# Softmax sums in two parts and subtractions in three, set between dependent additions; logarithms two tiles later

## Chip, cores, metric

One NeuronCore of a Trainium2 chip. The time is device microseconds (us) of one execution; lower is better. A program on one core has no second die to compare with, so a run counts as slow when it lies over 1.5% above the fastest of the same kernel.

## The reference

```python
# dynamic convolution: x (8, 4160, 192), weight_gen (8, 4160, 8 heads, 7 taps)
w = softmax(weight_gen, axis=-1)                    # over the 7 taps
out[b, s, h, :] = sum over k of w[b, s, h, k] * x_pad[b, s + k, h, :]
# then, on the 33280 rows x of 192:
h1, h2 = x @ w1, x @ w2                             # 192 -> 1024
return np.maximum(h1, h2) @ w_out                   # 1024 -> 192
```

## The kernel before

The 260 rows of each partition are 17 batches (the last has 4 rows). A batch is worked off in units of 8 rows (the first two and the last batch in units of 4). TensorE (PE) takes a unit of 8 rows in 8 tiles, each with an eighth of the hidden layer. Per unit, VectorE (DVE) multiplies the 7 shifted copies of x by the weights and adds the 7 products in three steps; a transposing DMA turns the result y_t into yt; PE makes the hidden layer and the output from it; ScalarE (ACT) does the Relu, evacuates, and makes the weights as exp(w - ln(sum of exp w)). So each batch also needs one sum over the taps (`red`) and one subtraction of its logarithm (`shift`) on DVE, and one `ln` and three exponentials on ACT.

```python
    def red(b):                                   # L132: 896 fp32 elements to 128
        ...
        nc.vector.reduce_sum(out=s_ts[b], in_=_sub(e_ts.pop(b), 0, [[K, TH], [1, K]]), axis=AX.X)
    def ln(b):                                    # L135, ScalarE
        nc.scalar.activation(out=s_ts[b], in_=s_ts[b], func=AF.Ln)
    def shift(b):                                 # L140: 896 fp32 elements
        ...
        nc.vector.tensor_tensor(out=w_t, in0=w_t, in1=..., op=ALU.subtract)
    def adds(b, o, first=False):                  # L172, L177, L179: each reads what the one before wrote
        ...
        nc.vector.tensor_tensor(out=taps(0, 1, 3), in0=taps(0, 1, 3), in1=taps(3, 1, 3), op=ALU.add)
        ...
        nc.vector.tensor_tensor(out=taps(0, 2, 2), in0=taps(0, 2, 2), in1=taps(1, 5, 2), op=ALU.add)
        nc.vector.tensor_tensor(out=_sub(y_ts[b], ...), in0=taps(0, 1, 1), in1=taps(2, 1, 1), op=ALU.add)
    ...
    def extra(t):                                 # what goes with tile t of PE; s = its place in the batch
        if s == 0 and b + 1 < NB:
            mul(c, 0); shift(c + 1); adds(c, 0)   # c = b + 1
        if s == 8 and b + 2 < NB:
            mul(b + 1, 8); red(b + 3); adds(b + 1, 8)
        ...
        for o, at in ((0, 8), (8, 12)):           # the two exponentials that make the weights
            c = (t - at) // 16 + 2
            if (t - at) % 16 == 0 and ...: weights(c, o)
        if s == 14 and 3 < b + 3 < NB:
            ln(b + 3)
        c = (t - 4) // 16 + 3                     # the exponential ahead of the sums
        if (t - 4) % 16 == 0 and 3 < c < NB:
            exp_sum(c)
```

PE takes its tiles in groups of three. An even group evacuates four results and calls `extra` between its Relus ("large" below); an odd one evacuates two and calls it at its end ("small").

The softmax here doesn't subtract the row's maximum and nothing guards it: scores larger than these inputs give would overflow.

Of the kernel before, what the change touches and what calls it, by code (L numbers as in the profile page):

```python
# [9 lines left out]
FP32 = mybir.dt.float32  # L10
# [4 lines left out]
AX = mybir.AxisListType  # L15


def _sub(base: bass.AP, off: int, dims):
    ap = [list(base.ap[0])] + [[int(s), int(c)] for s, c in dims]
    return dataclasses.replace(base, offset=base.offset + off, ap=ap)  # L20
# [3 lines left out]
def kernel(  # L24
# [9 lines left out]
    nc = tc.nc  # L34

    B, S, D = x.shape
    H, K = weight_gen.shape[2], weight_gen.shape[3]
    F = moe_w1.shape[1]
    P = 128
# [9 lines left out]
    BATCHES = [(c, min(16, CPP - c)) for c in range(0, CPP, 16)]  # L49
    NB = len(BATCHES)  # L50


    def pieces(b):
        n = BATCHES[b][1]
        at, done = [], 0
        for w in (4, 4, 4, 4) if b < 2 else (8, 8) if n == 16 else (n,):
            at.append((done, w))
            done += w
        return at
# [18 lines left out]
    psm = ctx.enter_context(tc.tile_pool(name="psm", bufs=3))  # L78
# [19 lines left out]
    wg_ts, xb_ts, e_ts, s_ts, en_ts, y_ts, yt_ts = {}, {}, {}, {}, {}, {}, {}  # L98
# [26 lines left out]
    def exp_sum(b):  # L125
        e_ts[b] = pe_.tile([P, BATCHES[b][1] * WGC], FP32, name="e_t", tag="e")
        nc.scalar.activation(out=e_ts[b], in_=wg_ts[b], func=AF.Exp)  # L127

    def red(b):
        TH = BATCHES[b][1] * H  # L130
        s_ts[b] = psm.tile([P, TH], FP32, name="sum_t", tag="sum")
        nc.vector.reduce_sum(out=s_ts[b], in_=_sub(e_ts.pop(b), 0, [[K, TH], [1, K]]), axis=AX.X)  # L132

    def ln(b):
        nc.scalar.activation(out=s_ts[b], in_=s_ts[b], func=AF.Ln)  # L135

    def shift(b):
        TH = BATCHES[b][1] * H
        w_t = _sub(wg_ts[b], 0, [[K, TH], [1, K]])
        nc.vector.tensor_tensor(out=w_t, in0=w_t, in1=_sub(s_ts.pop(b), 0, [[1, TH], [0, K]]),  # L140
                                op=ALU.subtract)

    def weights(b, o):

        N = dict(pieces(b))[o] * H
        if b not in en_ts:
            en_ts[b] = pen.tile([P, 16 * WGC * 2], BF16, name="en_t", tag="en")
        nc.scalar.activation(  # L148
            out=_sub(en_ts[b], o * WGC * 2, [[2 * N, K], [2, N], [1, 2]]),
            in_=_sub(wg_ts[b], o * WGC, [[1, K], [K, N], [0, 2]]), func=AF.Exp,  # L150
        )


    def mul(b, o):

        n = dict(pieces(b))[o]
        nc.vector.tensor_tensor(  # L157
            out=m_t[:, K * o * D:K * (o + n) * D],
            in0=_sub(xb_ts[b], o * D, [[D, K], [1, n * D]]),
            in1=_sub(en_ts[b], o * WGC * 2, [[2, K * n * H], [0, G // 2], [1, 2]]),  # L160
            op=ALU.mult,
        )

    def adds(b, o, first=False):

        w = dict(pieces(b))[o]
        n = w * D

        def taps(at, step, cnt):
            return _sub(m_t, K * o * D + at * n, [[step * n, cnt], [1, w * D]])  # L170

        nc.vector.tensor_tensor(out=taps(0, 1, 3), in0=taps(0, 1, 3), in1=taps(3, 1, 3), op=ALU.add)  # L172
        if first:
            return
        if b not in y_ts:
            y_ts[b] = py.tile([P, 16 * D], BF16, name="y_t", tag="y")
        nc.vector.tensor_tensor(out=taps(0, 2, 2), in0=taps(0, 2, 2), in1=taps(1, 5, 2), op=ALU.add)  # L177

        nc.vector.tensor_tensor(  # L179
            out=_sub(y_ts[b], o * D, [[64, 2], [P, 3 * w // 2], [1, 64]]),  # L180
            in0=taps(0, 1, 1), in1=taps(2, 1, 1), op=ALU.add,
        )

    def transpose(u):

        b, o, n = UNITS[u]
        yt = pyt.tile([P, 8 // 2 * 3 * P], BF16, name="yt", tag="yt")
        nc.sync.dma_start_transpose(
            out=yt[:, 0:n // 2 * 3 * P].rearrange("p (b t) -> p b t", t=P),
            in_=y_ts[b][:, o * D:(o + n) * D],  # L190
        )
        yt_ts[u] = yt

        nc.gpsimd.tensor_copy(out=gate, in_=yt[:, 0:1])  # L194
        c = b + 1 if o == 0 else b + 2
        if o == 8 and c < NB:
            load_x(c, 0, min(8, BATCHES[c][1]))
        if o == 0 and c < NB and BATCHES[c][1] > 8:
            load_x(c, 8, BATCHES[c][1] - 8)
        if o == 0 and b + 3 < NB:  # L200
            load_wg(b + 3, nc.gpsimd)
# [167 lines left out]
    OUTS, c = [[], [], []], 0  # L369
    for g in range(3, len(GROUPS)):  # L370
        most = 4 if g == 3 else 2 if GROUPS[g][1] == 2 or len(OUTS[-1]) == 4 else 4
        n = min(most, ready[g] - c)
# [80 lines left out]
    with tc.tile_pool(name="pstage", bufs=1) as pstage:  # L453
# [7 lines left out]
        for p0, p1, eng in ((16, P, nc.sync), (1, 16, nc.gpsimd)):  # L461
            eng.dma_start(
                out=xs[p0:p1, 0:PAD * D],
                in_=bass.AP(tensor=x.tensor, offset=(p0 * CPP - PAD) * D,
                            ap=[[CPP * D, p1 - p0], [1, PAD * D]]),
# [30 lines left out]
        nc.vector.tensor_copy(out=ident, in_=ident_f)  # L496
        exp_sum(0)
        red(0)
        ln(0)
        shift(0)  # L500
        xb_ts[0] = pxb.tile([P, (16 + PAD) * D], BF16, name="xb_t", tag="xb")
        nc.scalar.activation(out=xb_ts[0][:, 0:PAD * D], in_=xs[:, 0:PAD * D], func=AF.Copy,
                             scale=msk[:, 0:1])
        for o in (0, 4, 8, 12):
            weights(0, o)
        nc.vector.tensor_copy(out=xb_ts[0][:, PAD * D:(PAD + 4) * D],
                              in_=xs[:, PAD * D:(PAD + 4) * D])
# [5 lines left out]
        def w_diff(h, copy):  # L513
# [15 lines left out]
            out=wo[:, :].rearrange("p (f d) -> p f d", d=D),  # L529
            in_=bass.AP(tensor=moe_w_out.tensor, offset=0, ap=[[D, P], [P * D, FCH], [1, D]]),  # L530
# [39 lines left out]
        w_diff(1, nc.vector.tensor_copy)  # L570
        mul(0, 8)
        adds(0, 8, True)
        sum_transpose(1)
        exp_sum(1)
        red(1)
        hidden(1)
        ln(1)
        shift(1)
        mul(0, 12)
        tp = w1_transposed()  # L580
# [22 lines left out]
        weights(1, 4)  # L603
        mul(1, 0)
        adds(1, 0, True)
        sum_transpose(2, LEFT)
        load_x(2, 0, 16)
# [3 lines left out]
        w10_product()  # L611
        exp_sum(2)
        red(2)
        adds(1, 4, True)
        sum_transpose(3)
        weights(1, 8)
# [6 lines left out]
    def rest_of_1():  # L623
        mul(1, 8)
        shift(2)
        adds(1, 8, True)
        mul(1, 12)
# [16 lines left out]
    def extra(t):  # L644

        u, k = TILES[t]
        b, o, n = UNITS[u]
        s = o + k
        if s == 0 and b + 1 < NB:

            c = b + 1
            mul(c, 0)
            if c + 1 < NB:
                shift(c + 1)
            adds(c, 0)
        if s == 8 and b + 2 < NB:
            mul(b + 1, 8)
            if b + 3 < NB:
                red(b + 3)
            adds(b + 1, 8)  # L660
        if k == n // 4 - 1 and 7 < u + 1 < NU:
            transpose(u + 1)

        for o, at in ((0, 8), (8, 12)):
            c = (t - at) // 16 + 2
            if (t - at) % 16 == 0 and 2 < c < NB and o in dict(pieces(c)):
                weights(c, o)
        if s == 14 and 3 < b + 3 < NB:
            ln(b + 3)
        c = (t - 4) // 16 + 3  # L670
        if (t - 4) % 16 == 0 and 3 < c < NB:
            exp_sum(c)
# [7 lines left out]
    for g in range(4, len(GROUPS)):  # L680
        if GROUPS[g][1] == 3 and "c" not in ps:
            later_ps()
        tiles = [t for t in range(GROUPS[g][0], sum(GROUPS[g])) if t >= 16]
        if g in early:
            hidden(g, OUTS[g], early[g][0])
            early[g][1]()
            for t in tiles:
                extra(t)
        else:
            hidden(g, OUTS[g], beside=lambda: [extra(t) for t in tiles])  # L690
# [30 lines left out]
```

## Time and profile before

418.81 us median of 4 runs (418.5 to 419.28); profiled span 417.0 us.

| | busy us | ends |
|---|---|---|
| TensorE (PE) | 403.7 | with the kernel |
| VectorE (DVE), last y_t | 378.0 | 385.07 us |
| ScalarE (ACT) | 359.8 | with the kernel |

A high busy share on three engines does not tell which sets the time. The chain of work that ended last is followed back from the end; at each step it goes to what released an instruction, or to the one before it on its engine. On the kernel before it stayed on DVE:

```profile
DVE 73%; PE 17%; issue 4%; ACT 3%; DMA 2%; SPq 1%; DVEq 0%
```

### The profile page before, as it was taken

To read this page: it belongs to the slowest core of one execution; us is meant where nothing else is said; L and a number is where in the kernel's file an instruction comes from. 1 tells how busy PE (TensorE), PEld (TensorE's weight loads), DVE (VectorE), ACT (ScalarE), POOL (GpSimd) and SP (SyncE) were. 2 spreads that over 40 slices of the span, in tenths; PEclk is the share of its full clock that TensorE was granted. 3 is DMA by queue.
4 is the path that set the end of the run, shared out by engine and by line. 5 is a ranking of instruction groups with operands and counts; after the bars stand their busy time and mean duration, and the time that the engine had idled before them with its cause. 6 is when DMAs were issued, how large, how long until landed. Compare 5 with 4: busy or idle time off the path is not lost.

```text
span 417.0 us, 15881 instructions
## 1 busy us (share of the span) xinstructions
PE 403.7 (97%) x7369; PEld 326.8 (78%) x7369; DVE 378.0 (91%) x177; ACT 359.8 (86%) x416; POOL 69.0 (17%) x102
## 2 busy tenths in 40 slices
PE   7989999999999999999999999999999999999995
PEld 7878899777777778777787777877778677777795
DVE  5999999999999999999999999999999999999000
ACT  5898989999999899898989899899998898887871
POOL 1510101221201122212112232200113221120000
PEclk9999999999999999999999999999999999999999
DMA  8965427867569756875866669557674787685213
GB/s 235 260 168 169 108 68 169 183 153 129 144 151 181 192 151 163 207 147 153 201 149 147 168 127 242 142 163 198 142 209 64 165 202 151 128 163 115 97 49 144
DMA packets 60242, 65.68 MB, mean 157 GB/s; under 512 B 47601, under 2 KB 48497, under 8 KB 60176
## 3 DMA queue, kind: packets, MB, share of 16 engines
q0 software_dynamic: 8128, 24.11, 28.3%
q1 hardware_dynamic: 46720, 15.30, 21.5%
q10 hardware_dynamic: 5328, 25.27, 15.8%
q8 instruction: 57, 0.93, 0.9%
q14 instruction: 9, 0.07, 0.1%
HBM read 35.96 MB, written 25.56 MB: 148 GB/s over the span
## 4 chain that ended last, share of the span: by engine, by line
DVE 73%; PE 17%; issue 4%; ACT 3%; DMA 2%; SPq 1%; DVEq 0%
DVE m_t L157 36%; DVE m_t L172 15%; DVE m_t L177 11%; PE op_ps L290 8%; PE hd L250 5%; DVE sum_t L132 3%; DVE y_t L179 3%; DVE wg_t L140 3%; DMA ws1T<-in_moe_w_dram 2%; PE op_ps L302 2%; ACT rd_t L260 1%; PE hdp L250 1%; PE yps L218 1%; ACT en_t L148 0%; SPq L480 0%
## 5 line engine op out<-in xcount | busy, mean ns | idle before, releaser
L260 ACT ACTIVATE rd_t<-hd 128x1024 bf16<-128x1024 f32 (+1 forms) x206 | 234.6, 1183 | 30.8 <-PE hd L250 30.3
L290 PE MATMUL op_ps<-wo,rd_t 64*128 64x192 bf16 x4160 | 210.3, 243 | 0.1
L290 PEld LDWEIGHTS <-rd_t 64*128 64x128 bf16 x4160 | 180.1, 94 | 16.2 <-ACTq L323 0.3
L250 PE MATMUL hd<-yt,wd 64*128 64x512 bf16 (+1 forms) x1584 | 187.2, 360 | 1.1 <-ACT rd_t L260 0.9
L157 DVE TENSOR_TENSOR m_t<-xb_t,en_t 128x10752 bf16<-128x10752 bf16 (+1 forms) x37 | 187.5, 5070 | 0.2 <-ACT en_t L148 0.2
L250 PEld LDWEIGHTS <-wd 64*128 64x128 bf16 x1776 | 92.8, 94 | 42.3 <-issue 1.4
L194 POOL CAST gate<-yt 128x1 f32<-128x1 bf16 x29 | 33.2, 1146 | 280.8 <-DMA yt<-y_t 280.8
L172 DVE TENSOR_TENSOR m_t<-m_t 128x4608 bf16<-128x4608 bf16 (+1 forms) x34 | 79.5, 2339 | 0.1
L346 ACT COPY o_t<-op_ps 128x384 f32<-128x384 f32 (+1 forms) x99 | 56.9, 585 | 8.2 <-PE op_ps L290 8.1
L302 PE MATMUL op_ps<-w,yt 64*128 64x192 bf16 x780 | 55.3, 243 | 3.2 <-ACT o_t L346 2.5
L302 PEld LDWEIGHTS <-yt 64*128 64x128 bf16 x780 | 38.6, 94 | 20.1 <-issue 5.6
L177 DVE TENSOR_TENSOR m_t<-m_t 128x3072 bf16<-128x3072 bf16 (+1 forms) x29 | 50.2, 1730 | 1.0
L148 ACT ACTIVATE en_t<-wg_t 128x896 bf16<-128x896 f32 (+1 forms) x37 | 34.1, 935 | 1.9 <-ACT o_t L346 1.2
L179 DVE TENSOR_TENSOR y_t<-m_t 128x1536 bf16<-128x1536 bf16 (+1 forms) x29 | 27.4, 944 | 1.0
L336 DVE COPY o_t<-op_ps 128x192 f32<-128x192 f32 x1 | 0.4, 358 | 27.9 <-ACT o_t L336 27.9
L115 POOL DMA_DIRECT2D xb_t<-in_x_dram x32 | 17.2, 539 | 24.8 <-DVE m_t L157 16.1
L132 DVE TENSOR_REDUCE sum_t<-e_t 128x128 f32<-128x896 f32 (+1 forms) x17 | 17.6, 1037 | 2.9 <-ACT e_t L127 2.9
L127 ACT ACTIVATE e_t<-wg_t 128x896 f32<-128x896 f32 (+1 forms) x17 | 15.8, 928 | 3.3 <-DMA wg_t<-in_weight_gen_dram 2.8
L140 DVE TENSOR_TENSOR wg_t<-wg_t,sum_t 128x896 f32<-128x896 f32 (+1 forms) x17 | 17.7, 1043 | 0.8 <-ACT sum_t L135 0.8
L260 ACT ACTIVATE rd_t<-hdp 128x1024 bf16<-128x1024 f32 x16 | 15.7, 1027 | 1.5 <-PE hdp L250 0.5
L218 PE MATMUL yps<-ident,m_t 128*64 128x128 bf16 x492 | 15.3, 220 | 0.3 <-DVE m_t L157 0.2
L218 PEld LDWEIGHTS <-m_t 128*64 128x64 bf16 x492 | 14.1, 110 | 1.9 <-issue 1.1
(45 smaller groups left out, 85.6 us busy)
## 6 DMA issues: line engine op xcount, KB each, us to landing
out_dram<-o_t ACTq DMA_DIRECT2D x28, 768.0 KB, 4.3
xb_t<-in_x_dram POOLq DMA_DIRECT2D x28, 384.0 KB, 4.9
wg_t<-in_weight_gen_dram POOLq DMA_DIRECT2D x14, 448.0 KB, 6.3
xb_t<-xb_t POOLq DMA_DIRECT2D x16, 288.0 KB, 5.4
out_dram<-o_t ACTq DMA_DIRECT2D x8, 384.0 KB, 3.2
wg_t<-in_weight_gen_dram SPq DMA_DIRECT2D x2, 448.0 KB, 5.3
xs<-in_x_dram SPq DMA_DIRECT2D x2, 384.0 KB, 6.8
xb_t<-in_x_dram POOLq DMA_DIRECT2D x1, 768.0 KB, 6.8
```

The costliest lines, as they stand in the source:

```text
L148: nc.scalar.activation(out=_sub(en_ts[b], o * WGC * 2, [[2 * N, K], [2, N], [1, 2]]), in_=_sub(wg_ts[b], o * WGC, [[1, K], [K, N], [0, 2]] ...
L157: nc.vector.tensor_tensor(out=m_t[:, K * o * D:K * (o + n) * D], in0=_sub(xb_ts[b], o * D, [[D, K], [1, n * D]]), in1=_sub(en_ts[b], o * W ...
L172: nc.vector.tensor_tensor(out=taps(0, 1, 3), in0=taps(0, 1, 3), in1=taps(3, 1, 3), op=ALU.add)
L177: nc.vector.tensor_tensor(out=taps(0, 2, 2), in0=taps(0, 2, 2), in1=taps(1, 5, 2), op=ALU.add)
L179: nc.vector.tensor_tensor(out=_sub(y_ts[b], o * D, [[64, 2], [P, 3 * w // 2], [1, 64]]), in0=taps(0, 1, 1), in1=taps(2, 1, 1), op=ALU.add,)
L194: nc.gpsimd.tensor_copy(out=gate, in_=yt[:, 0:1])
L218: nc.tensor.matmul(yps[half(j), k * P:(k + 1) * P], lhsT=m_t[:, at:at + 64], rhs=ident, start=(t == taps[0]), stop=(t == taps[-1]), skip_g ...
L250: nc.tensor.matmul(hid_out(t, f, j), lhsT=wd[half(j), s * F + f * P:s * F + (f + 1) * P], rhs=_sub(yt_ts[u][half(j), :], (s + j) % 3 * P, ...
L260: nc.scalar.activation(out=rd[:, k * 1024:(k + n) * 1024], in_=hd[:, at:at + n * 1024], func=AF.Relu)
L290: return nc.tensor.matmul(op_out(c), lhsT=rd[half(r), k * 1024 + at:k * 1024 + at + P], rhs=wo[half(r), f * D:(f + 1) * D], start=False, s ...
L302: nc.tensor.matmul(op_out(c + j), lhsT=yt_ts[u][half(j), (3 * i + (s + j) % 3) * P:(3 * i + (s + j) % 3 + 1) * P], rhs=w10[half(j), s * D: ...
L346: nc.scalar.copy(out=_sub(o, c % 24 * D, [[D, len(qs)], [h * D, 2], [1, D]]), in_=_sub(tile_, at + (qs[0] - p) * D, [[D, len(qs)], [512, 2 ...
```

## The change

The intent: DVE's three additions wait for each other's results. An independent piece of the softmax work set between two of them should hide that wait. The sum is cut in two (ahead of the first and second addition), the subtraction in three (ahead of each). As a sum is then complete later, the logarithms are moved from tile 14 of a batch to tile 16 (tile 0 of the next), for batches 6 to 16.

```diff
-    def red(b):
-        ...
+    def red(b, i=0, of=1):
+        if i == 0:
+            s_ts[b] = psm.tile([P, BATCHES[b][1] * H], FP32, name="sum_t", tag="sum")
+        hs, at, ap = part(b, i, of)
+        nc.vector.reduce_sum(out=s_ts[b][:, hs], in_=_sub(e_ts[b], at, ap), axis=AX.X)
-    def shift(b):
+    def shift(b, i=0, of=1):        # the same with hs, at, ap = part(b, i, of)
-    def adds(b, o, first=False):
+    def adds(b, o, first=False, beside=lambda i, of: None):
+        beside(0, 3)
         (first addition)
+        beside(1, 3)
         (second addition)
+        beside(2, 3)
         (third addition)
@@ extra(t)
+        at = 14 if t <= 16 * 3 else 16
+        c = (t - at) // 16 + 3
+        if (t - at) % 16 == 0 and 3 < c < NB:
+            ln(c)
-            if c + 1 < NB:
-                shift(c + 1)
-            adds(c, 0)
+            adds(c, 0, beside=lambda i, of: shift(c + 1, i, of) if c + 1 < NB else None)
-            if b + 3 < NB:
-                red(b + 3)
-            adds(b + 1, 8)
+            adds(b + 1, 8, beside=lambda i, of: red(b + 3, i, 2) if b + 3 < NB and i < 2 else None)
-        if s == 14 and 3 < b + 3 < NB:
-            ln(b + 3)
```

(`part` gives the slice of rows; other lines cut.)

More of the change, by code (lines that the diff above doesn't have):

```diff
@@ L127, in exp_sum, with part @@
         nc.scalar.activation(out=e_ts[b], in_=wg_ts[b], func=AF.Exp)
-    def red(b):
-        TH = BATCHES[b][1] * H
-        s_ts[b] = psm.tile([P, TH], FP32, name="sum_t", tag="sum")
-        nc.vector.reduce_sum(out=s_ts[b], in_=_sub(e_ts.pop(b), 0, [[K, TH], [1, K]]), axis=AX.X)
+    def part(b, i, of):
+        n = BATCHES[b][1]
+        h0, h1 = n * i // of * H, n * (i + 1) // of * H
+        return slice(h0, h1), h0 * K, [[K, h1 - h0], [1, K]]
+    def red(b, i=0, of=1):
[3 more added lines that the diff above has]
+        nc.vector.reduce_sum(out=s_ts[b][:, hs], in_=_sub(e_ts[b], at, ap), axis=AX.X)
     def ln(b):
         nc.scalar.activation(out=s_ts[b], in_=s_ts[b], func=AF.Ln)
-    def shift(b):
-        TH = BATCHES[b][1] * H
-        w_t = _sub(wg_ts[b], 0, [[K, TH], [1, K]])
-        nc.vector.tensor_tensor(out=w_t, in0=w_t, in1=_sub(s_ts.pop(b), 0, [[1, TH], [0, K]]),
+    def shift(b, i=0, of=1):
+        hs, at, ap = part(b, i, of)
+        w_t = _sub(wg_ts[b], at, ap)
+        nc.vector.tensor_tensor(out=w_t, in0=w_t, in1=_sub(s_ts[b], hs.start, [[1, hs.stop - hs.start], [0, K]]),
                                 op=ALU.subtract)
```

## The prediction

> **What bounds the kernel now.** I read the page first: busy shares, then the slices.
>
> ```profile
> PE 403.7 (97%) x7369; PEld 326.8 (78%) x7369; DVE 378.0 (91%) x177; ACT 359.8 (86%) x416; POOL 69.0 (17%) x102
> ...
> PE   7989999999999999999999999999999999999995
> PEld 7878899777777778777787777877778677777795
> DVE  5999999999999999999999999999999999999000
> ```
>
> Three engines are nearly full. VectorE (DVE) has no idle slice until about 385 us and then nothing to do; TensorE (PE) goes on to the end. The chain of work that ended last is mostly DVE (73%), which suggests that every us saved there is a us off the time. I don't believe that, because of the next view, the waits of PE:
>
> ```profile
> PE op_ps L302 <- ACT o_t L346: 2.5, 6, 0.5
> PE hd L250 <- ACT rd_t L260: 0.9, 3, 0.3
> ...
> PE hd L250 <- DMA yt<-y_t: 0.2, 1, 0.2
> ```
>
> DVE's product reaches PE through the transposing DMA that writes yt. PE waited for it once, 0.2 us. So after the start PE sets the time, and DVE only nearly does. To see how nearly, I counted the weight loads of wd tile by tile in the trace and set the first one of each unit against the landing of that unit's yt (the start of the GpSimd copy gate, which waits for nothing else). The lead shrinks from 10.45 us (unit 8) to 6.0 (unit 21), 1.6 (units 27 and 28), 0.18 (29), nothing (30), 3.1, 1.5, 0.5, 2.8, 1.1 and 10.6 (units 31 to 36). DVE needs 11.92 us for a unit of 8 tiles, PE about 11.6, so PE has just caught up.
>
> The same count gives PE's own stalls: two groups of three tiles take 8.59 us when nothing waits. From 58 tiles on the excesses are: 1.09 us (from 110.89 us), 0.14 (137.77), 0.62 (180.85), 0.14 (207.26), 0.63 (250.34), 0.14 (276.79), 1.10 (319.86), 0.48 (346.67). The timeline of ScalarE (ACT) tells what two of these kinds are:
>
> ```profile
> 209.00 1.88 ACT L260 ACTIVATE rd_t<-hd 128x2048 bf16<-128x2048 f32 x1 [0.27 <-PE hd L250]
> 210.90 1.03 ACT L148 ACTIVATE en_t<-wg_t 128x896 bf16<-128x896 f32 x1
> 211.83 0.30 ACT L135 ACTIVATE sum_t<-sum_t 128x128 f32<-128x128 f32 x1
> 212.03 1.01 ACT L260 ACTIVATE rd_t<-hd 128x1024 bf16<-128x1024 f32 x1
> 212.94 0.80 ACT L346 COPY o_t<-op_ps 128x768 f32<-128x768 f32 x1
> ...
> 350.17 1.04 ACT L148 ACTIVATE en_t<-wg_t 128x896 bf16<-128x896 f32 x1
> 351.73 0.23 ACT L135 ACTIVATE sum_t<-sum_t 128x32 f32<-128x32 f32 x1 [0.53 <-DVE sum_t L132]
> 351.87 1.01 ACT L260 ACTIVATE rd_t<-hd 128x1024 bf16<-128x1024 f32 x1
> ```
>
> A logarithm (L135) behind an exponential, inside a group that evacuates four results, makes the last Relu late: 0.14 us on PE, three times. The last logarithm moreover waits 0.53 us for its sum on DVE while ACT's queue stands: 0.48 us on PE. The 0.62 to 0.63 come from two exponentials close together; the first 1.09 has 0.46 more, as an exponential waited 0.42 us for DVE to free its buffer. The 1.10 is 0.63 plus 0.47 for the late yt of unit 30.
>
> **What the skill says.** (1) The Trainium skill, "Perfetto Trace Analysis", section "Optimizing Scalar/DVE Operations": some 60 ns of data access per DVE instruction on SBUF, and a profiled latency about twice that, since the write acknowledgement lies beside the next instruction. (2) The same page's section "DVE / Act Engine Instruction": the recorded end is when the write is acknowledged, and semaphores go up after that; so a reader of the result waits for the acknowledgement, an independent instruction doesn't. (3) "VectorE: DVE Perf Modes", "Rules for kernel authors", says of chained operations to minimize their count, not the semaphores, as the pipe drains regardless. The trace agrees with (1) and (2), not with (3):
>
> ```profile
> 202.61 5.75 DVE L157 TENSOR_TENSOR m_t<-xb_t,en_t 128x10752 bf16<-128x10752 bf16 x1
> 208.28 1.08 DVE L132 TENSOR_REDUCE sum_t<-e_t 128x128 f32<-128x896 f32 x1
> 209.28 2.55 DVE L172 TENSOR_TENSOR m_t<-m_t 128x4608 bf16<-128x4608 bf16 x1
> 211.86 1.76 DVE L177 TENSOR_TENSOR m_t<-m_t 128x3072 bf16<-128x3072 bf16 x1
> 213.65 0.96 DVE L179 TENSOR_TENSOR y_t<-m_t 128x1536 bf16<-128x1536 bf16 x1
> 214.53 5.75 DVE L157 TENSOR_TENSOR m_t<-xb_t,en_t 128x10752 bf16<-128x10752 bf16 x1
> ```
>
> Start to start, the product takes 5.67 us though its record lasts 5.75: the independent sum behind it starts 0.08 us before its end. The second addition reads the first's result and starts 0.03 us after its end (211.86 against 209.28 + 2.55). A dependent neighbour thus costs 0.11 us more than an independent one.
>
> (4) The rate in "VectorE: DVE Perf Modes", "Specifications", 0.96 GHz, gives the fixed part: 10752 elements at two a cycle are 5.60 us, so 0.07 are left of 5.67; the sum, 896 at one a cycle, is 0.933 us and takes 1.00, again 0.07.
>
> **The change part by part.** The built program has 41 more DVE instructions: 14 subtractions (batches 3 to 16) in three parts and 13 sums (batches 4 to 16) in two. TensorE's list is the same, apart from waits; ACT's has the same instructions with 8 of the logarithms in other places.
> - *A unit with a subtraction.* Two more instructions, 2 x 0.07 = 0.14 us more; both boundaries between additions get an independent part, 2 x 0.115 = 0.23 less. Net -0.09 us, x14 = -1.3.
> - *A unit with a sum.* One more instruction, +0.07; one boundary, -0.115 (the third addition still follows the second directly). Net -0.045, x13 = -0.6.
> - Sum for DVE: 1.9 us earlier at the end, some 1.5 at unit 30. I take off up to 0.4 for logarithms that now come just in time: that of batch 7 should end near 148.5 us with its subtraction due at 148.3, and batches 5 and 6 have 0.1 to 0.2 us to spare.
> - *Logarithms.* From batch 6 on they are due two tiles later; for batches 8, 11, 14 these tiles lie in the same group, so nothing moves. Batches 7, 10, 13 leave the crowded group for the end of a small one, where ACT waited some 0.4 us for PE anyway: -0.14 x 3 = -0.42 on PE. Batch 16 leaves too, and its sum is then long there: -0.48. Batches 6, 9, 12, 15 go into a group that evacuates four but has no exponential: 0.3 us where ACT waited 0.58 (333.55 us), so nothing lost.
> - *PE and yt.* At unit 30 DVE gains 1.5 less up to 0.4, PE at most 0.7 by then; the lead of -0.47 us becomes slightly positive: -0.3 to -0.47.
> - *First exponential at 113.06 us:* its buffer comes free 0.2 to 0.3 us sooner: -0.2.
>
> Sum on PE's path: -(0.42 + 0.48 + 0.35 + 0.2) = -1.45 us. 418.8 - 1.45 = 417.35; I say **417.4 us**.
>
> **The rivals.**
> - *DVE is the bound, as the chain says:* all 1.9 us come off, and perhaps the logarithms' 0.9 as well: 416.0 to 416.9. Against it: PE waited 0.2 us for DVE's output in the whole run, and the tail from 352 us runs at PE's 8.59 a pair.
> - *Splitting only adds overhead,* if the wait isn't hidden by a part of 0.3 to 0.5 us, or the skill's advice on counts holds: 41 x 0.07 = 2.9 us more on DVE. As the lead at units 29 to 35 is about 1 us, PE would wait for most of it: 420.5 to 421. Against it: the 0.11 is measured on every unit, and the shortest part, 280 elements, lasts far longer than the 0.11 us to hide.
> - *The subtraction ends later and ACT waits for it.* The last part ends 5.3 us after the first begins, not 1.0. For batch 15 the exponential came at 341.58, the subtraction at 339.40; waiting for all would cost ACT some 1.3 us and PE 0.7. But the built program gives the second exponential of a batch a wait on DVE that it didn't have, so the first waits for the first two parts only, ended 3.2 us after the start: 339.40 - 1.5 + 3.2 = 341.1. It fits by 0.5 us. If it doesn't: 418.
> - *The transposes land just as late* since their 4 to 7.5 us from y_t to landing follow the other traffic: the 0.35 stays, 417.8.
>
> **Range and chances.** The logarithms' 0.9 us I hold near certain, the other 0.55 likely. Runs of the kernel before spread over 0.8 us. Range 416.5 to 418.8. No mechanism reaches 8 us: within 2% at 0.98, the other two at 0.01 each.
>
> **What would show it.** Right: add-to-add boundaries with a part between start 0.08 us before the record's end; a unit takes 11.83 us with a subtraction and 11.88 with a sum; DVE's last y_t ends near 383.5, not 385.07; the excesses of 0.14 and 0.48 and PE's wait for yt are gone, those of 0.62 stay. Wrong: units of 11.92 us or more (nothing hidden); en_t waiting for wg_t on ACT; DVE waiting for sum_t by more than 0.5 us in all; a time below 416.5, which would mean that PE follows DVE after all.

## The result, and the profile after

418.27 us median of 4 runs (418.01 to 418.48) against 418.81: 0.54 us less. The ratio is 0.9986 with a 95% interval of 0.9969 to 1.0003, so by the runs alone the two are the same. (Here and below a ratio is the mean time of one kernel's fast runs over that of the other's of the same rounds, so not quite the ratio of the medians.) The changed kernel run again on another chip gave 418.19 against 418.60, ratio 0.9985 (0.9967 to 1.0002).

| us | before | changed |
|---|---|---|
| profiled span | 417.03 | 416.70 |
| DVE: unit with a subtraction / with a sum | 11.92 / 11.92 | 11.81 / 11.85 |
| DVE: last y_t ends | 385.07 | 383.33 |
| PE: from the first weight load of tile 58 to that of the last unit | 287.80 | 286.95 |
| PE: first weight load of the last unit | 398.68 | 397.87 |
| last store issued | 413.37 | 412.56 |
| last store landed (end of its last data packet) | 415.31 | 414.93 |

The row of PE's stretch leaves the start of the run out: in the 14 profiles PE came to tile 58 at 110.1 to 111.2 us, so that spans alone differ by up to 1 us for a reason that no run here explains. I use this stretch of PE in the experiments too.

The timeline of DVE in the changed kernel (start, duration, line, shapes), a unit with a subtraction and the second half of one with a sum:

```profile
196.31 2.55 DVE L181 TENSOR_TENSOR m_t<-m_t 128x4608 bf16<-128x4608 bf16 x1
198.78 0.44 DVE L147 TENSOR_TENSOR wg_t<-wg_t,sum_t 128x280 f32<-128x280 f32 x1
199.14 1.75 DVE L187 TENSOR_TENSOR m_t<-m_t 128x3072 bf16<-128x3072 bf16 x1
200.81 0.50 DVE L147 TENSOR_TENSOR wg_t<-wg_t,sum_t 128x336 f32<-128x336 f32 x1
201.23 0.95 DVE L190 TENSOR_TENSOR y_t<-m_t 128x1536 bf16<-128x1536 bf16 x1
202.09 5.75 DVE L164 TENSOR_TENSOR m_t<-xb_t,en_t 128x10752 bf16<-128x10752 bf16 x1
...
210.76 0.61 DVE L139 TENSOR_REDUCE sum_t<-e_t 128x64 f32<-128x448 f32 x1
211.29 1.74 DVE L187 TENSOR_TENSOR m_t<-m_t 128x3072 bf16<-128x3072 bf16 x1
213.07 0.96 DVE L190 TENSOR_TENSOR y_t<-m_t 128x1536 bf16<-128x1536 bf16 x1
```

The first addition takes 2.47 us from its start to the next start, where it took 2.58; the second 1.67 where a part follows and 1.78 where the third addition follows directly. So each hidden boundary is worth 0.11 us, as forecast, and the parts are long enough.

The waits of PE (who waited for whom, us in total, times, longest), the rows that answer to those of before:

```profile
PE op_ps L313 <- ACT o_t L357: 2.2, 5, 0.5
PE hd L261 <- ACT rd_t L271: 0.9, 3, 0.3
```

The row with yt is gone. The chain has turned over too, though the time hardly moved:

```profile
PE 73%; ACT 14%; DVE 5%; issue 3%; DMA 2%; SPq 1%; ACTq 0%; DVEq 0%
```

DVE's 73% before and PE's 73% now come from the same near-tie. As I read it, just one wait of PE for DVE late in the run, or one logarithm of ACT that waits for DVE, is enough to lead the chain over to DVE; and DVE has no gap there in which the chain could leave it again.

PE's excess over 8.59 us for a pair of groups, by first tile of the pair, counted from the weight loads as in the prediction:

| first tile | 58 | 76 | 106 | 124 | 154 | 172 | 202 | 220 |
|---|---|---|---|---|---|---|---|---|
| before | 1.09 | 0.14 | 0.62 | 0.14 | 0.63 | 0.14 | 1.10 | 0.48 |
| changed | 1.09 | 0.14 | 0.63 | 0.14 | 0.64 | 0.14 | 0.64 | none |

Two things went: 0.46 us at tile 202 (the wait for yt of unit 30) and 0.48 at tile 220 (the last logarithm). ACT's timeline at the latter:

```profile
349.84 1.04 ACT L155 ACTIVATE en_t<-wg_t 128x896 bf16<-128x896 f32 x1
350.78 1.01 ACT L271 ACTIVATE rd_t<-hd 128x1024 bf16<-128x1024 f32 x1
...
356.66 0.23 ACT L142 ACTIVATE sum_t<-sum_t 128x32 f32<-128x32 f32 x1 [0.41 <-ACT o_t L357]
```

The Relu follows the exponential at once; the logarithm comes 5 us later and finds its sum. But the excesses of 0.14 us stayed. At tile 124 the logarithm did leave the group:

```profile
210.97 1.03 ACT L155 ACTIVATE en_t<-wg_t 128x896 bf16<-128x896 f32 x1
211.91 1.01 ACT L271 ACTIVATE rd_t<-hd 128x1024 bf16<-128x1024 f32 x1
```

Compared with the lines in the prediction (210.90 to 212.03), nothing stands between exponential and Relu any more, and PE's 0.14 us is the same. So it was not the logarithm's.

PE is 0.81 us earlier at its last unit and issues the last store 0.81 us earlier. The span is only 0.33 us shorter: the store takes 2.38 us to land instead of 1.95.

### The profile page after: what moved, and what is told of

Read it like the earlier page. It is cut to its first block, busy times and chain, and to the rows that moved or that the text cites. A ratio compares the mean times of both kernels' runs of the same rounds, so it can differ in the third digit from the quotient of the medians.

```text
span 416.7 us, 15916 instructions
## 1 busy us (share of the span) xinstructions
PE 402.9 (97%) x7369; PEld 326.2 (78%) x7369; DVE 377.3 (91%) x218; ACT 360.1 (86%) x416; POOL 69.2 (17%) x102
## 4 chain that ended last, share of the span: by engine, by line
PE 73%; ACT 14%; DVE 5%; issue 3%; DMA 2%; SPq 1%; ACTq 0%; DVEq 0%
PE op_ps L301 34%; PE hd L261 31%; ACT rd_t L271 8%; PE op_ps L313 7%; ACT en_t L155 3%; DVE m_t L164 2%; DMA xs<-in_x_dram 2%; ACT o_t L357 2%; PE yps L229 1%; PE hdp L261 1%; DVE m_t L181 1%; ACT e_t L127 1%; SPq L491 1%; ACTq L367 0%; DVE m_t L187 0%
## 5 line engine op out<-in xcount | busy, mean ns | idle before, releaser
L205 POOL CAST gate<-yt 128x1 f32<-128x1 bf16 x29 | 34.2, 1179 | 278.4 <-DMA yt<-y_t 278.4
L147 DVE TENSOR_TENSOR wg_t<-wg_t,sum_t 128x280 f32<-128x280 f32 (+4 forms) x45 | 22.0, 489 | 1.2 <-ACT sum_t L142 1.0
L139 DVE TENSOR_REDUCE sum_t<-e_t 128x64 f32<-128x448 f32 (+2 forms) x30 | 19.6, 653 | 2.7 <-ACT e_t L127 2.7
L127 ACT ACTIVATE e_t<-wg_t 128x896 f32<-128x896 f32 (+1 forms) x17 | 15.8, 928 | 3.1 <-DMA wg_t<-in_weight_gen_dram 2.6
```

The source lines that it names most:

```text
L205: nc.gpsimd.tensor_copy(out=gate, in_=yt[:, 0:1])
```

## The experiments

Twelve runs in four calls, those of a call on one chip, with 11 or 12 executions of the kernel before beside them. Of 49 executions of the kernel before (the four at first included) six were above 419.5 us; medians hide that, so I give each run's executions.

### 1. The split alone (e1_split_only)

```diff
-        at = 14 if t <= 16 * 3 else 16      # the changed kernel, logarithms back at tile 14
...
+        if s == 14 and 3 < b + 3 < NB:
+            ln(b + 3)
```

> The sums and subtractions split as in the change, the logarithms left where they were. My theory (TensorE sets the time, the vector engine only nearly): the vector engine ends its last y_t about 1.7 us earlier than in the kernel before, TensorE's wait for yt at unit 30 goes (-0.47 us), but the last logarithms now wait for the second half of their sums (that of batch 16 some 1.3 us, that of batch 13 some 0.6), and TensorE loses 1 to 1.4 us there and 0.3 us for batch 13: 418.8 to 419.8 us, that is 0.0 to +1.0 against before. Rival (the vector engine is the bound): -1.5 to -1.9 us, 417.0. Rival (only the place of the logarithms mattered): 418.8, with TensorE's stall near tile 220 as before, 0.48.

Measured: 418.99 us (418.88 to 419.11), ratio 1.0007 (0.9995 to 1.0020). DVE's last y_t ended at 382.66 us, 2.4 us earlier than before (0.5 of them already there at 59 us), and PE never waited for yt. It lost 0.87 us at tile 220 and 0.52 more at tile 172, where ACT's logarithms waited for the second halves of their sums (idle before it and releaser in brackets):

```profile
281.73 0.31 ACT L142 ACTIVATE sum_t<-sum_t 128x128 f32<-128x128 f32 x1 [0.50 <-DVE sum_t L139]
...
352.02 0.23 ACT L142 ACTIVATE sum_t<-sum_t 128x32 f32<-128x32 f32 x1 [0.93 <-DVE sum_t L139]
```

PE's stretch from tile 58 is 288.33 us, 0.53 longer than before. A DVE 1.9 us faster and a kernel no faster: what the split gives to yt, ACT's queue takes back, and the move of the logarithms is what makes the split harmless.

### 2. The logarithms alone (e2_logs_only)

The kernel before with the `ln` lines of the change, sums and subtractions whole.

> The logarithms moved as in the change, nothing split. My theory: TensorE's stall of 0.48 us near tile 220 goes, its wait for yt at unit 30 (0.47 us) stays or grows a little; -0.4 us, 418.4. The stalls of 0.14 us near tiles 76, 124 and 172 stay, as the trace after the change says that they are not the logarithms'. Rival (the vector engine is the bound): 418.8, no change, since its last y_t ends at 385.1 as before. Rival (the split gave nothing): -0.54 us as the whole change.

Measured: 418.00, 418.22, 418.26, 419.25, 423.27, 423.39 us. The median, 418.75, is not a fair summary of two groups; the ratio is 1.0037 (0.9988 to 1.0086). The three fastest lie where the changed kernel lies. In the trace (of the 419.25) the stall at tile 220 is gone, the 0.14 us at tiles 76, 124 and 172 are still there, and PE waited for yt at units 23, 30 and 33, the longest time 0.7 us, as the leads there are zero without the split. The last logarithm's 0.48 us is thus the move's. But in this trace the wait for yt at unit 30 grew from 0.47 to 0.95 us, so PE's stretch is 287.86 us, no shorter than before. What the split adds in an execution whose transposes land in time does not show in the times; this trace shows where it would.

### 3. Only the subtractions split (e3_sub_only)

`red(b + 3)` whole ahead of the first addition; the rest as changed.

> Only the subtractions in three parts, the sums whole, the logarithms moved. My theory: a unit with a subtraction takes 11.81 us, one with a sum 11.92; the vector engine ends at 385.07 - 14 x 0.1 = 383.7 us; the lead of unit 30 is just positive, so TensorE gains the same 0.9 us as with the whole change: 418.3. Rival (each us of the vector engine counts): between the whole change and the logarithms alone, in proportion to the vector engine's end.

Measured: 418.33, 418.44, 418.48, 418.87, 420.00 us. Units take 11.81 (subtraction) and 11.92 us (sum), the last y_t ends at 383.40, PE has no wait for yt and the lead of unit 30 is 2.05 us. The profiled span, 416.5, is about that of the whole change (416.7), and by the times the halved sums bought nothing. The trace says otherwise: its start was 0.48 us earlier, and PE's stretch is 287.30 us, 0.35 longer than in the changed kernel. It lost 0.21 us at tile 214 and 0.14 at tile 220, because ACT's first exponential for batch 15 waited for the second part of the subtraction, the third of my rivals:

```profile
340.78 0.44 DVE L147 TENSOR_TENSOR wg_t<-wg_t,sum_t 128x280 f32<-128x280 f32 x1
341.26 1.03 ACT L155 ACTIVATE en_t<-wg_t 128x896 bf16<-128x896 f32 x1 [0.52 <-DVE wg_t L147]
```

In the changed kernel the same two only just fit: the part ends at 341.22 and the exponential starts at 341.25, without a wait. There is no margin left.

```profile
340.77 0.45 DVE L147 TENSOR_TENSOR wg_t<-wg_t,sum_t 128x280 f32<-128x280 f32 x1
341.25 1.03 ACT L155 ACTIVATE en_t<-wg_t 128x896 bf16<-128x896 f32 x1
```

### 4. DVE without the subtractions (e4_no_sub; wrong result)

```diff
             mul(c, 0)
-            if c + 1 < NB:
-                shift(c + 1)
             adds(c, 0)
```

> The kernel before without the subtractions of batches 3 to 16: the result is wrong on purpose. The vector engine has 14 us less to do. My theory (TensorE sets the time): only TensorE's wait for yt goes, -0.47 us, perhaps the 0.48 us of the last logarithm as well: 417.9 to 418.4. Rival (the vector engine is the bound, as the chain of work that ended last said with 73%): -10 us or more, below 409.

Measured: 418.25 us (418.11 to 418.74), ratio 0.9992 (0.9980 to 1.0004). The page's busy row:

```profile
PE 403.6 (97%) x7369; PEld 327.5 (79%) x7369; DVE 366.2 (88%) x163; ACT 359.8 (86%) x416; POOL 64.6 (15%) x102
```

DVE's last y_t ended at 373.87 us, 11 us earlier than before (0.7 of them from the start of the run; a unit without its subtraction takes 11.05 us instead of 11.92, so the 14 us that I expected were some 10.5), and the time fell by about what the small change reached too. PE's stretch is 286.91 us, that of the changed kernel (286.95). This settles it: DVE is not the bound of the kernel before, against 73% of the chain.

### 5 to 7. ACT's exponentials spread (e5_spread_before, e6_spread_after, e7_spread_three), with the changed kernel again (e8_after_again)

If PE's stalls of 0.62 us came off, would DVE's time begin to count? The same two edits of `extra` were made on the kernel before (e5), on the changed one (e6), and on the changed one with the sums in three parts (e7):

```diff
-        for o, at in ((0, 8), (8, 12)):
+        for o, at in ((0, 8), (8, 13)):
...
-        c = (t - 4) // 16 + 3
-        if (t - 4) % 16 == 0 and 3 < c < NB:
+        at = 2 if (t - 16) % 48 == 2 else 4
+        c = (t - at) // 16 + 3
+        if (t - at) % 16 == 0 and (t - 16) % 48 != 4 and 3 < c < NB:
             exp_sum(c)
```

> The changed kernel again, on the same chip as the three beside it: -0.54 us against before, 418.3, whatever the theory.

> The kernel before with the scalar engine's work spread: the second exponential of each batch due one tile later, and the exponential ahead of the sums two tiles earlier in every third batch. So no two of them follow each other around the evacuation of four results. My theory: TensorE's stalls of 0.62 (near tiles 106, 154, 202) and 0.14 us go, 2.3 us in all, but then it runs into the vector engine: the lead of yt is 0 to 2 us at units 29 to 35, so nearly all of it comes back as waits for yt: 418.3 to 418.8, 0 to -0.5 us. Rival (TensorE and the scalar engine set the time, the vector engine has room): -2.3 us, 416.5.

> The same spreading on the changed kernel. My theory: the leads at units 29 to 35 are 1.4 to 4.6 us there, so TensorE may gain about 1.4 us before it waits for yt: -1.4 against the changed kernel, 416.9, and the split is worth 1.3 us or more here against the same spreading on the kernel before. Rival (the vector engine's time is worth nothing): equal to the same spreading on the kernel before.

> The spreading on the changed kernel, with the sums in three parts too, so that every boundary between additions has an independent part. My theory: 13 x (0.11 - 0.07) = 0.5 us less on the vector engine, as far as yt still holds TensorE back: 416.5 to 416.9. Rival (fixed costs win): 0.5 us slower than with the sums in two parts.

Measured: e8 418.02 to 418.34. e5 418.90 to 421.75. e6 417.53, 417.54, 418.34, 418.89, and two of 427.5 (slow). e7 420.82 to 423.70, and one of 437.44 (slow). None of it is the -1.4 us expected; the two best of e6 are 0.5 us below the best of e8. The edit was bad, and the trace of e7 shows why: the exponential that I had moved two tiles earlier came before its input.

```profile
194.78 0.95 ACT L127 ACTIVATE e_t<-wg_t 128x896 f32<-128x896 f32 x1 [2.44 <-DMA wg_t<-in_weight_gen_dram]
```

ACT's queue stands, PE stands behind it, and then PE is slow as well: in e5 PE was idle for 3.75 us until 267.83, and the clock records have half speed for 3.4 us from 267.1. I drop these runs as a test of DVE. They do tell what the 0.14 us are: in e6 they are gone at tiles 76, 124 and 172, and 0.29 us stand at tiles 64, 112 and 160 instead, the pairs into which the exponential ahead of the sums (L127) was moved; e5 agrees up to its long stall at tile 160. In runs e11 and e12 below, which have the other half of the edit only, the 0.14 are back. So they belong to that exponential (0.98 us, at 199.88 in the changed kernel), which stands at the end of a small group one pair of groups before the pair that loses. By which waits it reaches PE so much later I did not follow.

### 8. One exponential one tile later, with and without the split (e11_later_after, e12_later_unsplit)

```diff
-        for o, at in ((0, 8), (8, 12)):
+        for o, at in ((0, 8), (8, 13)):     # on the changed kernel; on the one with the logarithms moved alone
```

> The changed kernel with one thing more: the second exponential of a batch due at tile 13 instead of 12, which by the built program moves it in four places only, from right behind another exponential to the end of the next small group (the earlier spreading failed because the other half of it, the sums' exponential two tiles early, ran into the load of its input: the scalar engine waited 2.4 us for it in the trace). My theory: TensorE's stalls of 0.63 us near tiles 106, 154 and 202 go and part of the 1.09 near tile 58, 1.9 to 2.3 us; the leads of yt at units 29 to 35 are 1.4 to 4.6 us, so TensorE gains 1.3 to 1.9 us before it waits for yt: 416.4 to 417.0. Rival (the vector engine's time is worth nothing): as far below the changed kernel as the unsplit one with the same addition is below before.

> The same addition to the kernel with the logarithms moved and nothing split. My theory: the same stalls of TensorE go, but the leads of yt at units 29, 30 and 33 are 0 to 0.2 us here, so most of the 1.9 us comes back as waits for yt: 417.7 to 418.3, at least 1 us above the split one. Rival (the vector engine's time is worth nothing): the same time as with the split.

Measured, sorted: with the split 417.44, 417.86, 418.08, 419.39, 419.42, 423.51; without 417.32, 418.70, 420.01, 421.38, 422.75, 426.12 (slow). By the fast runs both have ratios of 1.000 with intervals of 0.5%, so the timing doesn't separate them; six executions are too few for tails like these. The traces do. With the split, the stalls of 0.63 us at tiles 106, 154 and 202 went, and the 1.09 at tile 58 fell to 0.44: PE came to tile 214 2.4 us earlier than in the changed kernel's first trace (335.40 against 337.76), of which 0.3 were there by tile 58 already. On the way it lost 0.37 us at tile 190, where a logarithm waited 0.87 us for its sum. Then it lost 1.40 us, again to the third of my rivals: ACT's exponential for batch 15 waited for the second part of its subtraction.

```profile
340.59 1.02 ACT L155 ACTIVATE en_t<-wg_t 128x896 bf16<-128x896 f32 x1 [1.71 <-DVE wg_t L147]
```

From there on the leads of yt at units 31 and 33 are zero. So the faster PE does run into DVE, by the waits for a sum and for the weights first and then by yt. Without the split its leads are zero earlier, at units 24 and 27, and at unit 28 PE stood for 4 us:

```profile
308.50 1.47 PE L250 MATMUL hd<-yt,wd 64*128 64x512 bf16 x6 [4.06 <-DMA yt<-y_t]
```

That wait is not DVE's doing: y_t of unit 28 was ready at 297.69 us, 0.4 earlier than in the kernel before, but its transpose landed 10.9 us later, where 6.1 passed in the kernel before. What held the transpose up I did not find. The split would have given 1.5 us of room here (y_t at 296.18 in the other run), not the 4.4 that were missing.

The windows of this run show what follows (stretch, length, busy time of each engine, the granted clock of PE, DMA share, GB/s):

```profile
300.00:306.00 6.00, 4.45 (x80) 3.39 (x75) 6.00 (x3) 5.27 (x7) 0.00 (x0) 1.00 1.25 191
306.00:313.00 7.00, 4.50 (x42) 3.39 (x43) 6.93 (x4) 1.46 (x2) 1.25 (x3) 0.54 0.42 74
313.00:320.00 7.00, 7.00 (x116) 5.18 (x114) 6.96 (x4) 5.69 (x7) 3.17 (x3) 0.97 0.74 230
```

After 4.06 us of idling PE had half its clock for 6.8 us; the pair of groups took 6.63 us too long. The Trainium skill, "TensorE: Matmul & The Clock Gate", section "What's actually happening", says that PE falls to half its clock after an idle window. The runs agree: 3.75 us idle, then 3.4 us at 0.5 (e5); 4.06 us idle, then 6.8 us at 0.5; in 1.23 us of idling (this run with the split) the clock stayed at 1.0. So a late transpose is, by this one profile, one way in which an execution of these kernels comes to be some us late, and it fits the clocks of 0.990 to 0.996 that many late executions of the edited kernels show. It does not explain the kernel before: of its six late executions only one has such a clock (422.44 us, 0.995), the others 0.997 to 1.0 (423.39 us at 1.0), so what delayed them stays open. Whether the split makes such executions rarer stays open: for the changed kernel itself none of 9 was above 419.5, against 6 of 49 of the kernel before, but in the last run below, which has the same split, it was 2 of 6.

### 9. The subtractions in six parts (e9_six_parts)

```diff
-            adds(c, 0, beside=lambda i, of: shift(c + 1, i, of) if c + 1 < NB else None)
+            adds(c, 0, beside=lambda i, of: [shift(c + 1, 2 * i + j, 2 * of) for j in range(2)] if c + 1 < NB else None)
```

> The changed kernel with the subtractions in six parts, two ahead of each adding step: 3 more instructions in each of 13 units, and one more in the last. My theory: each costs 0.07 us and hides nothing more, so a unit with a subtraction takes 11.81 + 0.21 = 12.02 us and the vector engine ends 2.7 us later, at about 386; the leads at units 29 to 33 fall from 1.4 to 4.6 us to about -1 to +2, so TensorE waits some 1 us for yt: 419.0 to 419.6. Rival (the instruction's fixed cost is hidden behind the next one): no difference to the changed kernel, 418.2.

Measured: 420.16 to 421.73, median 420.52, ratio 1.0036 (1.0008 to 1.0065). A unit with a subtraction takes 12.02 us, exactly the 11.81 + 3 x 0.07: the fixed cost of an instruction that hides nothing is real. The time rose by more than I expected, and not by the wait that I expected: PE never waited for yt (the smallest lead at units 29 to 33 is 0.17 us), and DVE's last y_t ended at 384.94, not 386. ACT stood instead. PE lost 0.51 us at tile 190 behind a logarithm that waited for its sum, and 0.93 at tile 214 behind an exponential that waited for the weights:

```profile
307.20 0.31 ACT L142 ACTIVATE sum_t<-sum_t 128x128 f32<-128x128 f32 x1 [1.01 <-DVE sum_t L139]
...
342.54 1.04 ACT L157 ACTIVATE en_t<-wg_t 128x896 bf16<-128x896 f32 x1 [1.24 <-DVE wg_t L149]
```

PE's stretch is 288.64 us, 1.7 longer than in the changed kernel. The end of the run is 0.5 us longer as well: the packets with instructions that the next section is about came twice beside the last store, at 414.6 and 415.67 us.

### 10. The last store (e13_eight_copies)

In 13 profiles the landing of the last store, up to its last data packet, took either 1.94 to 1.95 or 2.37 to 2.38 us. The trace's packets of queue 14, which carry instructions, go with it: where the last of them came at 410 to 411 us the landing was short, where it came at 412.9 us or later, beside the store, it was long. And that went with the number of ACT's instructions in the trace, its semaphore waits included: 588 or 589 in three kernels with the short landing, 582 or 583 in the ten with the long one. The change gives ACT six waits fewer: 588 before, 582 after.

```diff
+    few = consts.tile([P, 9], FP32, name="few")
+    nc.vector.memset(few[:, 0:1], 0.0)
+    for k in range(8):
+        nc.scalar.copy(out=few[:, k + 1:k + 2], in_=few[:, 0:1])
```

> The changed kernel with eight copies of one column on the scalar engine at its start, where it waits 2.6 us for its first input; one of 128 x 1 should take some 0.2 us, so they fit. Theory: the last instruction fetch (a DMA of queue 14) comes when the scalar engine reaches a certain number of instructions. With 588 or 589 in the trace (before, the split alone, the spreading on before) it was at 410 us and the last store landed 1.95 us after its issue; with 582 or 583 (five other kernels of this study, the changed one among them) at 413.5 and 2.37 us. With 590 it should be at or before 410, and the landing 1.95: TensorE as in the changed kernel, 0.4 us off the end, 417.8. Rival (the landing has nothing to do with the fetch, or the fetch not with that count): 2.37 us, 418.2.

Measured in the profile: the last of these packets came at 407.0 us, the last store was issued at 412.69 and landed 1.96 us later; the span is 416.4. The overview of DMA issues (output, queue, times, size, us to landing) for the last two stores of the SyncE queue in the kernel before, in the changed kernel and in this one; these times run on to the last semaphore update, 0.35 to 0.4 us after the last data packet:

```profile
out_dram<-o_t SPq DMA_DIRECT2D x1, 192.0 KB, 2.6
...
out_dram<-o_t SPq DMA_DIRECT2D x1, 96.0 KB, 2.3
```

```profile
out_dram<-o_t SPq DMA_DIRECT2D x1, 192.0 KB, 3.2
...
out_dram<-o_t SPq DMA_DIRECT2D x1, 96.0 KB, 2.8
```

```profile
out_dram<-o_t SPq DMA_DIRECT2D x1, 192.0 KB, 2.7
...
out_dram<-o_t SPq DMA_DIRECT2D x1, 96.0 KB, 2.3
```

So 0.43 us of what PE gained was lost behind the last store, by an accident of counting. This rests on one profile with the packet moved on purpose, and on the other 13 agreeing. In the timing the eight copies are not separable: 417.75, 418.05, 418.16, 418.35, 419.51, 421.73, ratio 1.0008 (0.9981 to 1.0035); the fastest execution is 0.26 us below the changed kernel's fastest.

## Why the prediction was right or wrong

The measured 418.27 us lies in the range and the class is right; the point, 417.4, was 0.87 us too low, and the forecast saving of 1.45 us is 0.54. The range reached up to the time of the kernel before, so lying in it says nothing for the mechanism: 0.62 of the 1.45 us came from the two steps called wrong below.

- **PE sets the time, DVE only nearly.** Right, and shown by the run without the subtractions (11 us less DVE, nothing off beyond the change's own half us).
- **0.07 us for an instruction, 0.115 for a boundary.** Right: 11.81 and 11.85 us for units forecast at 11.83 and 11.88. The 0.07 was an estimate, worked out from the clock in "VectorE: DVE Perf Modes", section "Specifications"; here three more instructions cost 0.21 us (run 9). (The shortest part is not 280 elements: batch 16 has 4 rows and parts of 56. These took 0.21 us each and hid the 0.11 as well: the additions beside them take 2.47 and 1.67 us from start to start.) The last y_t ended at 383.33, forecast near 383.5. Late logarithms cost DVE about 0.6 us (units 12 and 16 took 12.05 and 12.18 us), a little more than the 0.4 that I took off.
- **The wait for yt, 0.35, and the last logarithm, 0.48.** Right in the trace of the changed kernel: 0.46 and 0.48. But the wait for yt is no fixed term: it hangs on when the transpose of unit 30 lands. When the changed kernel was profiled again, and in the run with the eight copies, PE just met it there (lead -0.02): DVE's y_t was as early as in the first profile, but the transpose took 8.7 and 8.8 us from its end to landing, where it had taken 7.0. So the fourth rival, that the transposes land just as late, came half true; PE's excess there stayed within 0.11 us of 0.63. And the logarithms alone gave three executions as fast as the whole change.
- **Three times 0.14 from logarithms in a crowded group.** Wrong. This step read a neighbour as a cause: the logarithm stood in the group that lost the 0.14, but with it gone the group lost as much. The spread exponentials (e5 and e6 against e11) put the 0.14 on the exponential ahead of the sums.
- **0.2 at the first exponential.** Wrong: the excess at tile 58 stayed 1.09 and the exponential still stood 0.41 us, although DVE's product ended 0.19 us sooner. On ACT's own queue the issue of a store (0.34 us) stands right in front of it and ends 0.05 us before it starts, in both kernels; the releaser named was not the last obstacle. Run 8 moved the second exponential of this group (at 115.81 us), and 0.64 of the 1.09 went, as at the other tiles; the first stayed, with its wait and with 0.44 us of excess. No run took that away, so what it is worth is not shown.
- **Not foreseen: the last store.** 0.43 us given back, because six waits fewer on ACT moved an instruction fetch to where the store was in flight.

The rivals: DVE as the bound and overhead alone are both refuted (runs 4 and 9). The third, that ACT waits for a later subtraction, doesn't occur in the changed kernel, but the margin of 0.5 us that I worked out was 0.03: the exponential came 0.3 us earlier than in the kernel before, at 341.25, and the part ended at 341.22, 0.1 later than worked out. With PE half a us earlier at that place (run 3), 2 us earlier (run 8) or with more parts (run 9) the wait came, at batch 15 as worked out.

In sum, PE's gain of 0.81 us at its last unit (the two excesses, 0.94, less 0.13 by small shifts), less 0.43 us at the last store, is 0.38; the spans differ by 0.33 and the medians by 0.54.

## What to carry to other kernels

Between additions that read each other, a piece of other work on the same engine (records of 0.21 to 0.61 us here) hides 0.11 us and costs 0.07 for being cut off; that pays only where this engine is waited for, so look first at who waits for its output and how the lead develops over the run. When a part of a result is made later, go through all its readers on in-order queues: here the logarithms had to move along, and the exponential was 0.03 us from the same fate. The last chain of a profile with two nearly tied engines is no evidence which one is worth speeding up; take some of its work out and time it.

## What the Trainium skill lacked or had wrong

- "VectorE: DVE Perf Modes", section "Rules for kernel authors", advises for chained operations to minimize the count and not the semaphores. Here units with one or two more instructions were shorter, 11.85 and 11.81 against 11.92 us, as each boundary freed of its dependence gave 0.11 us.
- "Perfetto Trace Analysis", section "Optimizing Scalar/DVE Operations", has about 60 ns for an instruction of DVE: these runs show 0.07 us (three more for 0.21), near it. What it lacks: an instruction that reads the result of the one in front of it pays 0.11 us on top (2.58 against 2.47 us). That can be worked out from the page, but isn't said.
- "Runtime: NRT & Kernel Launch", section "Instruction fetch mechanics", calls the cost of a fetch mostly hidden. Here one beside the last store went with 0.43 us more until it landed, and six ACT instructions more or fewer decided it.
